# Row sums and outputs tested on the chip, with a general softmax path behind a branch at the end

## The chip, the core and the metric

The kernel runs on one core of a Trainium2 chip. The core has five engines that run side by side, each through its own instructions in order, and wait for each other by semaphores: TensorE (PE; its weight loads are listed as PEld), VectorE (DVE), ScalarE (ACT), GpSimd (POOL) and SyncE (SP, which only issues transfers and waits). The metric is the device time of one execution in microseconds; the numbers given are medians of several runs. One further execution is recorded by the hardware profiler; its span runs from the first to the last instruction of the program.

## The reference

Attention with keys that are also the values, pooled 4x4 from an image and projected, followed by a gated feed-forward block on every token.

```
q  [4, 12288, 128], kv [4, 384, 32, 128], w_sr [128, 128]
w_gate, w_val [128, 1536], w_out [1536, 128]

kv_pool = kv.reshape(B, H//4, 4, W//4, 4, C).mean(axis=(2, 4))
k = v = kv_pool.reshape(B, -1, C) @ w_sr              # 768 keys per image
s = (q @ k.T) / sqrt(C)
s = s - s.max(-1, keepdims=True)
a = exp(s);  a /= a.sum(-1, keepdims=True) + 1e-9
x = a @ v
out = (maximum(x @ w_gate, 0) * (x @ w_val)) @ w_out   # float32, [49152, 128]
```

## The kernel before

**Mathematics.** The kernel takes no maximum off the scores: it computes exp of the scaled scores in fp16 as it finds them, leaves the rows unnormalised through the values and both projections, and multiplies the output by the square of the inverse row sum, since gate and value each carry one factor of it. That is right as long as the scores are moderate.

**Tiles.** A tile is 512 tokens; there are NT = 96, in groups of GRP = 4, 24 tiles to each of the four images. A step k of the main loop (lines 811 to 865) works on four tiles at once in a software pipeline: scores and exp of tile k, values of tile k-2 (`kV`), the projections `v`, `y`, `g`, `h` of tile k-3 (`kF`), and the output projection of tile k-4 (`kO`). The order inside a step is written out by hand in the word lists STEADY, DRAIN and LAST (lines 100 to 111); nothing reorders it, because the schedule is manual (line 628). DRAIN serves the steps from k = 96 on, LAST the final one, k = 98. An `OPENING` list of words handles the first tiles while the first image's keys are still being built; its four lead tiles have transposed scores and get their row sums by a matmul with ones (`lead_sums`, `lead_inverse`, lines 467 to 498).

**Who does what.** For one tile, PE runs 8 score matmuls into the two-bank PSUM tile `wide` (line 397), 6 value matmuls (line 439), 12 value and 12 gate projections (lines 504, 515) and 12 output projections (line 545). ACT takes exp of a block of 128 tokens by 768 keys and has the row sum accumulated beside it into `a_sums` (line 402), and copies the value projections to fp16 (line 141 for `keep_value`). DVE does gate times value in one instruction (`gated`, line 523), the copy of the values (line 447), the reciprocal of a pair of tiles' row sums (`invert`, line 414) and a 32x32 block transpose of the output (line 553). POOL squares the inverse sums (416), spreads them over the partitions in 16 small copies a pair (423), multiplies the transposed output by them (line 558 in `out_turn`), pools the next images' keys (lines 256 to 264), and issues the loads of q and half of the output stores.

**The end.** Tiles 93 to 95 do not go through the transpose: their output projection runs token by token into PSUM (line 529), and `out_scale` multiplies there, on DVE for tile 93 and on ACT for tile 94; `out_store` stores. Tile 95 goes through `out_last`: three PSUM parts, the first two scaled by DVE (line 587), the last by ACT (line 585), each stored at once, the last from ACT's own queue. Then the program closes: SP waits for the stores, all engines meet, and the semaphores are cleared (instructions listed under line 894).

**Buffers.** `o_t` has two buffers, `o_sb` three, `wide` one. PSUM's other six banks are handed out by `bank` in the order in which they come free.

Of the kernel before, what the change touches and what calls it, by code (L numbers as in the profile page):

```python
# [9 lines left out]
FP32 = mybir.dt.float32  # L10
FP16 = mybir.dt.float16
AF = mybir.ActivationFunctionType
ALU = mybir.AluOpType
# [3 lines left out]
def kernel(  # L17
# [23 lines left out]
    nc = tc.nc  # L41

    B, N, C = q.shape
    _, H, W, _ = kv.shape
    r = 4
    J = (H // r) * (W // r)
    NJC = J // 128
    HC = H // NJC
    D_FF = moe_w_gate.shape[1]
    NFB = D_FF // 128  # L50
    T = 512
    NS = T // 128
    NST = N // T
    NT = B * NST
# [3 lines left out]
    X_SCALE = 512.0  # L58
    LEAD = GRP
    AT_BUFS = 4  # L60
    qk_scale = 1.0 / math.sqrt(C)

    assert C == 128 and N % T == 0 and J == 128 * NJC and D_FF == 128 * NFB
    assert NFB == 2 * NJC and NST % GRP == 0 and W // r == 8 and HC == 64
# [50 lines left out]
    const = ctx.enter_context(tc.tile_pool(name="const", bufs=1))  # L115
    work = ctx.enter_context(tc.tile_pool(name="work", bufs=2))
# [152 lines left out]
    sums, pixels = {}, {}  # L269
# [117 lines left out]
    def score_block(k, s):  # L387
        b = k // NST
        if s == 0:
            a16s[k] = work.tile([128, NS, J], FP16, tag="a16", bufs=4, name="a16")  # L390
            aTs[k] = work.tile([128, NJC, T], FP16, tag="aT", bufs=AT_BUFS, name="aT")
            if k % 2 == 0:
                a_sums[k // 2] = work.tile([128, 2, NS], FP32, tag="a_sums", bufs=2, name="a_sums")
        s_ps = s_banks[s] = wides[0].tile([128, 1024], FP32, tag="wide", name="wide_ps")
        qT = qTs[k // GRP][:, k % GRP * NS + s, :]
        for j0, j1 in ((0, 4), (4, NJC)):
            nc.tensor.matmul(  # L397
                s_ps[:, j0 * 128 : j1 * 128], qT, kv16[:, b, j0:j1, 0:C], start=True, stop=True
            )
# [87 lines left out]

    def lead_inverse():
        inverse = const.tile([128, NS * 4], FP32)
        nc.vector.reciprocal(inverse, x_banks.pop("turned")[:, :, 0])  # L490
        nc.vector.tensor_tensor(lead_square, inverse, inverse, op=ALU.mult)

    def lead_scales():
# [55 lines left out]
    def out_turn(k):  # L549


        o_t = work.tile([128, T], FP32, tag="o_t", bufs=2)
        nc.vector.transpose(o_t, freed(o_banks.pop(k)))  # L553
        o_sb = work.tile([128, 4, NS, 32], FP32, tag="o_sb", bufs=3)
        o_by = o_t.rearrange("t (s j c) -> t s j c", s=NS, j=4)
        to = o_sb.rearrange("t j s c -> t s j c")
        scale = scale_of(k).rearrange("t (s j o) -> t s j o", s=NS, o=1)
        nc.gpsimd.tensor_tensor(to, o_by, scale.to_broadcast([128, NS, 4, 32]), op=ALU.mult)  # L558
        del hTs[k]
        g = k // GRP  # L560
        rows = out[g * GRP * T : (g + 1) * GRP * T, :]
        moves = []
        for b in range(4):
            o_b = o_sb[32 * b : 32 * (b + 1)]
            if g == 0:
                to = rows.rearrange(
                    "(e j t i s) (b c) -> e b i j t s c", e=2, j=4, t=32, s=NS, c=32
                )
                moves += [(to[k // 2, b, k % 2, j], o_b[:, j]) for j in range(4)]
            elif g == NG - 1:  # L570
                to = rows.rearrange("(j t i s) (b c) -> b i j t s c", j=4, t=32, s=NS, c=32)
                moves += [(to[b, k % GRP, j], o_b[:, j]) for j in range(4)]
            else:
                to = rows.rearrange("(i t r) (b c) -> b i t r c", t=32, r=16, c=32)
                moves.append((to[b, k % GRP], o_b.rearrange("t j s c -> t (j s) c")))
        return moves
# [15 lines left out]
    def out_store(k, own, queue=nc.sync):  # L592
        queue.dma_start(
            out[k // GRP * GRP * T : (k // GRP + 1) * GRP * T, :].rearrange(
                "(p i s) c -> i p s c", p=128, i=GRP
            )[k % GRP][:, own], o_sbs[k][:, own],
        )
        if own.stop == NS:
            for tiles in (hTs, o_banks, o_sbs):
                del tiles[k]  # L600

    def out_last(k):
        parts = [bank([128, 2, 128]), bank([128, 1, 128]), bank([128, 1, 128])]
        owns = [slice(0, 2), slice(2, 3), slice(3, 4)]
        o_banks[k] = None

        def add(s, fb0, fb1):
            n = max(s - 1, 0)
            for fb in range(fb0, fb1):
                out_add(k, fb, s, parts[n][:, s - owns[n].start], fb == 0 and s != 1)  # L610

        def keep(n, engine, queue=nc.sync):
            out_scale(k, engine, owns[n], parts[n])
            out_store(k, owns[n], queue)

        held = NFB - 2
        add(0, 0, held)
        add(1, 0, held)
        add(2, 0, held)
        add(0, held, NFB)  # L620
        add(1, held, NFB)
        keep(0, nc.vector)
        add(2, held, NFB)
        keep(1, nc.vector)
        add(3, 0, NFB)
        keep(2, nc.scalar, nc.scalar)

    ctx.enter_context(tc.manual_schedule())

# [2 lines left out]
    make_identity(nc, ident)  # L632
    ident16 = const.tile([128, 128], FP16)
    nc.gpsimd.tensor_copy(ident16, ident)
    ones = const.tile([128, 32], FP16)
    nc.gpsimd.memset(ones, 1.0)
    lead_scale = const.tile([128, LEAD, NS * 4], FP32)
    nc.gpsimd.memset(kv16[:, :, :, 2 * C : 2 * C + 16], 1.0 / X_SCALE)

    w_sr_f32 = const.tile([128, C], FP32)  # L640
# [150 lines left out]
    def image_step(b, at, step):  # L791
        for pair in range(NJC // 2):
# [7 lines left out]
            elif since in (9, 11) and step == 1:  # L800
                turn_values_dma(b, 2 * pair + since // 11)

    for word in OPENING:
        word, _, number = word.partition("@")
        if number:
            asked.append(int(number))
        open_step(word)
        assert not asked
    usable[0] = 6
    last = NT + LAG - 1  # L810
    for k in range(LEAD + 2, last + 1):
        g, ph = divmod(k, GRP)
        if ph % 2:
            q_turn_two(g + 1, ph - 1)
        if ph:
            q_load(g + 2, [[0], [2], [3]][ph - 1])
        b = k // NST + 1
        at = k % NST - 4
        kO, kF, kV = k - LAG - 1, k - LAG, k - 2
        words = STEADY if k < NT else DRAIN if k < last else LAST  # L820
        for word in words:
            head, n = word.rstrip("0123456789"), int(word.lstrip("abcdefghijklmnopqrstuvwxyzADPT") or 0)
            if head == "o":
                out_proj(kO, n)
                if ph == 1 and n == NFB // 2:
                    q_load(g + 2, [1])
                for queue in (nc.gpsimd, nc.sync):
                    if out_moves and n >= 2:
                        queue.dma_start(*out_moves.pop())  # L829
                if spread:  # L830
                    spread_scales(*spread.pop(0))
                if b < B:
                    image_step(b, at, n)
            elif head == "oT":
                if kO < NT - 3:
                    out_moves.extend(out_turn(kO))
                elif k < last:
                    out_scale(kO, nc.vector, slice(0, NS))
                    out_store(kO, slice(0, NS))
            elif head in ("v", "y", "g", "h"):  # L840
                if kF < NT:
                    {"v": value_proj, "y": keep_value, "g": gate_proj, "h": gated}[head](kF, n)
            elif head in ("s", "e"):
                if k < NT:
                    {"s": score_block, "e": exp_block}[head](k, n)
                    if head == "e" and n % 2:
                        a_turn(k, n - 1, n + 1)
            elif head == "r":
                if LEAD < k <= NT and k % 2 == 0:
                    invert(k - 2)  # L850
                    spread += [(k - 2, j) for j in range(4)]
            elif head in ("tb", "P", "pk"):
                pair, since = divmod(at - 6 if head == "tb" else at - 8, 4)
                if b < B and 0 <= pair < NJC // 2 and since == 0:
                    if head == "tb":
                        moves.extend(turn_blocks(b, pair))
                    elif head == "P":
                        project(b, pair)
                    else:
                        keep_projected(b, pair)  # L860
            elif LEAD <= kV < NT:
                if head == "x":
                    values(kV, n)
                else:
                    keep_values(kV)
    out_scale(last - LAG - 1, nc.scalar, slice(0, NS))
    out_store(last - LAG - 1, slice(0, NS))
    out_last(last - LAG)


# [28 lines left out]
```

## Time and profile before

| | us |
|---|---|
| runs, median (lowest to highest of 3) | 1025.01 (1024.85 to 1026.36) |
| the profiled execution, its run | 1024.9 |
| its span | 1023.1 |
| PE busy | 1016.1 (99%) |
| ACT busy | 919.4 (90%) |
| DVE busy | 867.1 (85%) |
| POOL busy | 522.9 (51%) |
| PEld busy | 486.0 (48%) |

The granted TensorE clock was 1.0 throughout. How to read it: an engine's busy time counts its computing instructions, not its sequencer's waits and branches (POOL's issues of transfers are listed among its busy time here, as lines 162 and 829). Groups of instructions are named by their source line, with the tile that they write and those that they read and the shape as partitions x elements. The chain of waits is followed back from the last instruction to whatever released each one; its shares say which engine set the time. Most groups are the same in every tile: a tile's cast on ACT takes 596 ns on average, one gate-times-value on DVE 680 ns, an exp block 821 ns and its accumulator read 206 ns, the output scaling on POOL 1047 ns.

### The profile page before, as it was taken

How to read it: one execution, taken by the hardware profiler on the slowest of the kernel's cores; microseconds unless marked ns; L12 is line 12 of the kernel's file. 1: busy time of each engine (PE TensorE's matmuls, PEld its weight loads, DVE VectorE, ACT ScalarE, POOL GpSimd, SP SyncE). 2: the span in 40 equal slices, each digit the busy share in tenths (PEclk: the TensorE clock that was granted, in tenths of full speed). 3: DMA queues.
4: the chain of work that ended last, by engine and by line, in shares of the span. 5: the costliest groups of instructions: out<-in, count | busy, mean ns of one | idle time of the engine just before them, and what ended most of it. 6: DMA issues, size and time to landing. Idle time of an engine off the chain costs nothing.

```text
span 1023.1 us, 17486 instructions
## 1 busy us (share of the span) xinstructions
PE 1016.1 (99%) x5028; PEld 486.0 (48%) x5028; DVE 867.1 (85%) x1446; ACT 919.4 (90%) x1925; POOL 522.9 (51%) x1311
## 2 busy tenths in 40 slices
PE   8999999999999999999999999999999999999998
PEld 4444444444444444444444444444444444444445
DVE  4988888888888888888888888888888888888888
ACT  5999999999999999999999999999999999999986
POOL 3487857344347576544434856754434533443342
PEclk9999999999999999999999999999999999999999
DMA  9999998777898999788779899977686877767541
GB/s 320 172 170 183 187 202 145 141 124 127 138 199 159 182 189 174 130 123 145 122 135 200 167 173 199 159 131 133 127 131 114 149 120 129 124 121 123 102 87 44
DMA packets 475743, 153.48 MB, mean 150 GB/s; under 512 B 451584, under 2 KB 465920, under 8 KB 475648
## 3 DMA queue, kind: packets, MB, share of 16 engines
q1 hardware_dynamic: 453184, 126.08, 65.2%
q0 software_dynamic: 22032, 25.19, 16.4%
q10 hardware_dynamic: 432, 1.11, 0.3%
q8 instruction: 39, 0.64, 0.3%
q14 instruction: 56, 0.46, 0.2%
HBM read 53.94 MB, written 26.35 MB: 78 GB/s over the span
## 4 chain that ended last, share of the span: by engine, by line
PE 98%; DMA 1%; ACT 0%; DVE 0%; issue 0%; SPq 0%; DVEq 0%
PE bank_ps L504 24%; PE bank_ps L515 24%; PE bank_ps L545 24%; PE wide_ps L397 12%; PE bank_ps L439 12%; DMA kv_in<-in_kv_dram 1%; PE bank_ps L529 1%; PE bank_ps L456 0%; PE bank_ps L378 0%; PE wide_ps L336 0%; PE bank_ps L300 0%; PE bank_ps L314 0%; ACT aT L381 0%; PE bank_ps L474 0%; PE bank_ps L209 0%
## 5 line engine op out<-in xcount | busy, mean ns | idle before, releaser
L523 DVE SCALAR_TENSOR_TENSOR hT<-bank_ps,val 128x512 f16<-128x512 f32 x1152 | 728.2, 680 | 104.5 <-PE bank_ps L515 83.5
L141 ACT CAST val<-bank_ps 128x512 f16<-128x512 f32 x1149 | 629.1, 596 | 44.3 <-PE bank_ps L504 23.9
L504 PE MATMUL bank_ps<-xT,wv 128*128 128x512 f16 x1152 | 420.6, 379 | 0.0
L515 PE MATMUL bank_ps<-xT,wg 128*128 128x512 f16 x1152 | 376.3, 379 | 0.1
L545 PE MATMUL bank_ps<-hT,wo 128*128 128x512 f16 x1116 | 348.5, 379 | 0.0
L402 ACT ACTIVATE a<-wide_ps 128x768 f16<-128x768 f32 x368 | 302.0, 821 | 43.4 <-PE wide_ps L397 43.4
L397 PE MATMUL wide_ps<-kv,qT 128*128 128x512 f16 x736 | 179.7, 326 | 0.0
L439 PE MATMUL bank_ps<-aT,kv 128*128 128x512 f16 x552 | 178.9, 379 | 0.0
L558 POOL TENSOR_TENSOR o_sb<-o_t,scale 128x512 f32<-128x512 f32 x89 | 93.2, 1047 | 159.4 <-issue 142.0
L545 PEld LDWEIGHTS <-wo 128*128 128x128 f16 x1116 | 109.2, 98 | 131.9 <-issue 0.8
L515 PEld LDWEIGHTS <-wg 128*128 128x128 f16 x1152 | 112.7, 98 | 122.8 <-issue 0.8
L504 PEld LDWEIGHTS <-wv 128*128 128x128 f16 x1152 | 112.6, 98 | 105.5 <-issue 0.8
L423 POOL COPY scale<-square 32x8 f32<-32x8 f32 x736 | 141.2, 192 | 28.6
L416 POOL TENSOR_TENSOR square<-inverse 128x8 f32<-128x8 f32 x46 | 9.3, 202 | 248.0 <-DVE inverse L414 241.2
L829 POOL DMA_DIRECT2D out_dram<-o_sb x208 | 130.3, 632 | 9.9 <-POOL o_sb L558 7.4
L397 PEld LDWEIGHTS <-qT 128*128 128x128 f16 x736 | 72.0, 98 | 86.9 <-issue 0.2
L447 DVE CAST xT<-bank_ps 128x512 f16<-128x512 f32 x92 | 63.6, 692 | 32.0 <-PE bank_ps L439 32.0
L439 PEld LDWEIGHTS <-kv 128*128 128x128 f16 x552 | 54.0, 98 | 65.2
L402 ACT ACTIVATION_READ_ACCUMULATOR a<-wide_ps 128x1 f32 x368 | 76.0, 206 | 0.0
L553 DVE STREAM_TRANSPOSE o_t<-bank_ps 128x512 f32<-128x512 f32 x93 | 65.5, 704 | 0.0
L162 POOL DMA_DIRECT2D q<-in_q_dram x84 | 48.7, 581 | 0.3 <-issue 0.3
L256 POOL TENSOR_TENSOR s<-kv_in 128x512 f32<-128x512 f32 x36 | 45.1, 1283 | 0.7
(79 smaller groups left out, 204.9 us busy)
## 6 DMA issues: line engine op xcount, KB each, us to landing
kv_in<-in_kv_dram SPq DMA_DIRECT2D x42, 512.0 KB, 5.2
out_dram<-o_sb SPq DMA_DIRECT2D x177, 64.0 KB, 3.5
q<-in_q_dram POOLq DMA_DIRECT2D x88, 128.0 KB, 3.5
out_dram<-o_sb POOLq DMA_DIRECT2D x176, 64.0 KB, 4.1
aT<-a SPq DMA_TRANSPOSE x184, 4.4
kv_line<-in_kv_dram SPq DMA_DIRECT2D x4, 512.0 KB, 9.8
placed<-blocks SPq DMA_DIRECT2D x9, 128.0 KB, 2.4
kvT<-placed SPq DMA_DIRECT2D x36, 32.0 KB, 2.4
```

Source lines behind the costliest of these rows:

```text
L141: nc.scalar.copy(to, what)
L397: nc.tensor.matmul(s_ps[:, j0 * 128 : j1 * 128], qT, kv16[:, b, j0:j1, 0:C], start=True, stop=True)
L402: nc.scalar.activation(a16s[k][:, s, :], s_banks.pop(s)[:, 0:J], AF.Exp, scale=qk_scale, accum_out=a_sums[k // 2][:, k % 2, s : s + 1],)
L423: nc.gpsimd.tensor_copy(to[32 * b : 32 * (b + 1), :, :, j], squares[k // 2][32 * j : 32 * (j + 1)])
L439: nc.tensor.matmul(x_banks[k], kv16[:, k // NST, jc, C : 2 * C], aT[:, jc], start=first, stop=x_left[k] == 0,)
L504: nc.tensor.matmul(proj_banks["v", k, fb], wv16[:, fb * 128 : (fb + 1) * 128], xTs[k], start=True, stop=True,)
L515: nc.tensor.matmul(proj_banks["g", k, fb], wg16[:, fb * 128 : (fb + 1) * 128], xTs[k], start=True, stop=True,)
L523: nc.vector.scalar_tensor_tensor(hTs[k][:, fb, :], freed(proj_banks.pop(("g", k, fb))), 0.0, vals.pop((k, fb)), op0=ALU.max, op1=ALU.mult,)
L545: nc.tensor.matmul(o_banks[k], wo16[:, fb, :], hTs[k][:, fb, :], start=first, stop=o_left[k] == 0)
L553: nc.vector.transpose(o_t, freed(o_banks.pop(k)))
L558: nc.gpsimd.tensor_tensor(to, o_by, scale.to_broadcast([128, NS, 4, 32]), op=ALU.mult)
L829: queue.dma_start(*out_moves.pop())
```

## The change

The kernel now keeps every row's sum and tests on the chip whether its short cut was allowed, and has a second, general path for inputs where it was not.

- All row sums go to one constant tile `row_sums` (96 tiles x 4 sums per partition) instead of rotating buffers; the lead tiles' sums are copied there by POOL.
- After each tile's output is scaled, POOL adds one column of every 32 of it to a running tile `seen`, so that an infinity or a NaN stays visible. Tiles 93 and 94 are added in `out_store`.
- At the end of the step before the last (`oT` of k = 97), ACT runs Relu twice over all row sums, once for sums above 32 x 768 and once for sums below 768 / 8, and accumulates what is out of range (`sums_checked`).
- In `out_last`, DVE turns those accumulators and `seen` into flags (`seen_checked`, behind the last DVE scaling), and then the last tile's own outputs (`last_checked`, behind the last ACT scaling and store). A matmul with ones counts the flags over the partitions, a DVE maximum writes one integer, and all engines load that integer into a register.
- A branch runs `general()` if it is above zero: four loops of 24 iterations which compute every tile again, with each row's maximum taken off and the projections in fp32, one tile after the other. The branch is told that the side where nothing is done is the one to fall through.

The diff, with the inner part of the general path cut:

```diff
@@ -59,6 +59,7 @@
     LEAD = GRP
     AT_BUFS = 4
     qk_scale = 1.0 / math.sqrt(C)
+    SUM_MOST, SUM_LEAST = 32.0 * J, J / 8.0
 
     assert C == 128 and N % T == 0 and J == 128 * NJC and D_FF == 128 * NFB
     assert NFB == 2 * NJC and NST % GRP == 0 and W // r == 8 and HC == 64
@@ -390,7 +391,7 @@
             a16s[k] = work.tile([128, NS, J], FP16, tag="a16", bufs=4, name="a16")
             aTs[k] = work.tile([128, NJC, T], FP16, tag="aT", bufs=AT_BUFS, name="aT")
             if k % 2 == 0:
-                a_sums[k // 2] = work.tile([128, 2, NS], FP32, tag="a_sums", bufs=2, name="a_sums")
+                a_sums[k // 2] = row_sums[:, k : k + 2]
         s_ps = s_banks[s] = wides[0].tile([128, 1024], FP32, tag="wide", name="wide_ps")
         qT = qTs[k // GRP][:, k % GRP * NS + s, :]
         for j0, j1 in ((0, 4), (4, NJC)):
@@ -487,7 +488,9 @@
 
     def lead_inverse():
         inverse = const.tile([128, NS * 4], FP32)
-        nc.vector.reciprocal(inverse, x_banks.pop("turned")[:, :, 0])
+        sums_in = x_banks.pop("turned")[:, :, 0]
+        nc.gpsimd.tensor_copy(row_sums[:, 0:LEAD].rearrange("t e s -> t (e s)"), sums_in)
+        nc.vector.reciprocal(inverse, sums_in)
         nc.vector.tensor_tensor(lead_square, inverse, inverse, op=ALU.mult)
 
     def lead_scales():
@@ -556,6 +559,9 @@
         to = o_sb.rearrange("t j s c -> t s j c")
         scale = scale_of(k).rearrange("t (s j o) -> t s j o", s=NS, o=1)
         nc.gpsimd.tensor_tensor(to, o_by, scale.to_broadcast([128, NS, 4, 32]), op=ALU.mult)
+        nc.gpsimd.tensor_tensor(
+            seen, seen, o_sb[:, :, :, 0].rearrange("t j s -> t (j s)"), op=ALU.add
+        )
         del hTs[k]
         g = k // GRP
         rows = out[g * GRP * T : (g + 1) * GRP * T, :]
@@ -595,6 +601,10 @@
                 "(p i s) c -> i p s c", p=128, i=GRP
             )[k % GRP][:, own], o_sbs[k][:, own],
         )
+        if own.stop == NS and k < NT - 1:
+            nc.gpsimd.tensor_tensor(
+                seen[:, 0:NS], seen[:, 0:NS], o_sbs[k][:, :, 0], op=ALU.add
+            )
         if own.stop == NS:
             for tiles in (hTs, o_banks, o_sbs):
                 del tiles[k]
@@ -622,8 +632,11 @@
         keep(0, nc.vector)
         add(2, held, NFB)
         keep(1, nc.vector)
+        seen_checked()
         add(3, 0, NFB)
+        o_sb = o_sbs[k]
         keep(2, nc.scalar, nc.scalar)
+        last_checked(o_sb)
 
     ctx.enter_context(tc.manual_schedule())
 
@@ -632,9 +645,19 @@
     make_identity(nc, ident)
     ident16 = const.tile([128, 128], FP16)
     nc.gpsimd.tensor_copy(ident16, ident)
+    out_of_range = const.tile([1, 1], mybir.dt.int32)
     ones = const.tile([128, 32], FP16)
     nc.gpsimd.memset(ones, 1.0)
     lead_scale = const.tile([128, LEAD, NS * 4], FP32)
+    row_sums = const.tile([128, NT, NS], FP32)
+    too_much = const.tile([128, 1], FP32)
+    nc.gpsimd.memset(too_much, -SUM_MOST)
+    seen = const.tile([128, NS * 4], FP32)
+    nc.gpsimd.memset(seen, 0.0)
+    bad = const.tile([128, 2], FP32)
+    bad16 = const.tile([128, 22], FP16)
+    enough = const.tile([128, 1], FP32)
+    nc.gpsimd.memset(enough, SUM_LEAST)
     nc.gpsimd.memset(kv16[:, :, :, 2 * C : 2 * C + 16], 1.0 / X_SCALE)
 
     w_sr_f32 = const.tile([128, C], FP32)
@@ -800,6 +823,116 @@
             elif since in (9, 11) and step == 1:
                 turn_values_dma(b, 2 * pair + since // 11)
 
+    def sums_checked():
+        past = work.tile([128, NT * NS], FP32, tag="kv_s3", bufs=2, name="past")
+        sums = row_sums.rearrange("t k s -> t (k s)")
+        nc.scalar.activation(
+            past, sums, AF.Relu, scale=1.0, bias=too_much, accum_out=bad[:, 0:1]
+        )
+        nc.scalar.activation(past, sums, AF.Relu, scale=-1.0, bias=enough, accum_out=bad[:, 1:2])
+
+    def seen_checked():
+        nc.vector.tensor_scalar(bad16[:, 0:2], bad, 0.0, None, op0=ALU.is_gt)
+        nc.vector.tensor_scalar(
+            bad16[:, 2:18], seen, 0.0, 0.0, op0=ALU.mult, op1=ALU.not_equal
+        )
+
+    def last_checked(o_sb):
+        nc.vector.tensor_scalar(
+            bad16[:, 18:22], o_sb[:, :, 0], 0.0, 0.0, op0=ALU.mult, op1=ALU.not_equal
+        )
+        count = wides[0].tile([128, 1024], FP32, tag="wide", name="count_ps")
+        nc.tensor.matmul(count[0:1, 0:22], ones[:, 0:1], bad16, start=True, stop=True)
+        nc.vector.tensor_reduce(
+            out_of_range, count[0:1, 0:22], axis=mybir.AxisListType.X, op=ALU.max
+        )
+
+    def general():
+        def ps(n, shape, dtype=FP32):
+            return psum.tile(shape, dtype, tag=f"bank{n}", bufs=1, name="general_ps")
+
...
+        for b in range(B):
+            with tc.For_i(0, N, T) as n0:
+                q32 = work.tile([128, NS, C], FP32, tag="o_t", bufs=2, name="general_q32")
+                nc.sync.dma_start(
+                    q32, q[b, bass.ds(n0, T), :].rearrange("(p s) c -> p s c", s=NS)
+                )
...
+                    s_ps = wides[0].tile([128, 1024], FP32, tag="wide", name="general_wide")
+                    for j0, j1 in ((0, 4), (4, NJC)):
+                        nc.tensor.matmul(
+                            s_ps[:, j0 * 128 : j1 * 128], qT[:, s, :], kv16[:, b, j0:j1, 0:C],
+                            start=True, stop=True,
+                        )
+                    nc.vector.tensor_reduce(
+                        top[:, 0, s : s + 1], s_ps[:, 0:J], axis=mybir.AxisListType.X, op=ALU.max
+                    )
+                    nc.vector.tensor_scalar(
+                        top[:, 1, s : s + 1], top[:, 0, s : s + 1], -qk_scale, None, op0=ALU.mult
+                    )
+                    nc.scalar.activation(
+                        a16[:, s, :], s_ps[:, 0:J], AF.Exp, scale=qk_scale,
+                        bias=top[:, 1, s : s + 1], accum_out=total[:, 0, s : s + 1],
+                    )
+                    nc.vector.reciprocal(total[:, 1, s : s + 1], total[:, 0, s : s + 1])
+                    nc.vector.tensor_scalar(
+                        a16[:, s, :], a16[:, s, :], total[:, 1, s : s + 1], X_SCALE,
+                        op0=ALU.mult, op1=ALU.mult,
+                    )
...
+                o_sb = work.tile([128, NS, 128], FP32, tag="o_sb", bufs=3, name="general_o")
+                nc.vector.tensor_copy(o_sb, o_ps)
+                nc.sync.dma_start(
+                    out[bass.ds(n0 + b * N, T), :].rearrange("(p s) c -> p s c", s=NS), o_sb
+                )
+
     for word in OPENING:
         word, _, number = word.partition("@")
         if number:
@@ -832,6 +965,8 @@
                 if b < B:
                     image_step(b, at, n)
             elif head == "oT":
+                if k == last - 1:
+                    sums_checked()
                 if kO < NT - 3:
                     out_moves.extend(out_turn(kO))
                 elif k < last:
@@ -866,6 +1001,12 @@
     out_scale(last - LAG - 1, nc.scalar, slice(0, NS))
     out_store(last - LAG - 1, slice(0, NS))
     out_last(last - LAG)
+    flag = nc.values_load(
+        out_of_range[0:1, 0:1],
+        skip_runtime_bounds_check_because="it is a count of partitions that is only compared with 0",
+    )
+    with tc.If(flag > 0, preferred_fallthrough_block=False):
+        general()
 
 
 # ---- launch: one core; inputs and outputs as the reference has them ----
```

More of the change, by code (lines that the diff above doesn't have):

```diff
@@ new lines, in last_checked @@
+    def last_checked(o_sb):
[10 more added lines that the diff above has]
+            return psum.tile(shape, dtype, tag=f"bank{n}", bufs=1, name="general_ps")
+        wide32 = [
+            work.tile([128, 2, NFB, 128], FP32, tag="hT", bufs=3, name="wide32") for _ in range(2)
+        ]
+        wo32, wv32, wg32, h32 = [w[:, n] for w in wide32 for n in range(2)]
+        nc.vector.tensor_copy(wo32, wo16)
+        for to, w16 in ((wv32, wv16), (wg32, wg16)):
+            nc.vector.tensor_copy(to, w16.rearrange("c (fb f) -> c fb f", f=128))
+        for b in range(B):
[4 more added lines that the diff above has]
+                )
+                q16 = work.tile([128, NS, C], FP16, tag="val", bufs=6, name="general_q16")
+                nc.vector.tensor_copy(q16, q32)
+                qT_ps = ps(0, [128, NS, 128], FP16)
+                for s in range(NS):
+                    nc.tensor.transpose(qT_ps[:, s, :], q16[:, s, :], ident16)
+                qT = work.tile([128, NS, 128], FP16, tag="val", bufs=6, name="general_qT")
+                nc.vector.tensor_copy(qT, qT_ps)
+                a16 = work.tile([128, NS, J], FP16, tag="a16", bufs=4, name="general_a16")
+                aT = work.tile([128, NJC, T], FP16, tag="aT", bufs=AT_BUFS, name="general_aT")
+                total = work.tile([128, 2, NS], FP32, tag="general_sums", bufs=2)
+                top = work.tile([128, 2, NS], FP32, tag="square", bufs=3, name="general_top")
+                for s in range(NS):
+                    s_ps = wides[0].tile([128, 1024], FP32, tag="wide", name="general_wide")
[19 more added lines that the diff above has]
+                    )
+                aT_flat = aT.rearrange("k j t -> k (j t)")
+                nc.sync.dma_start_transpose(
+                    aT_flat.rearrange("k (x p) -> k x p", p=128), a16.rearrange("p s j -> p (s j)")
+                )
+                a_by = aT_flat.rearrange("k (s j p) -> k j s p", s=NS, j=NJC)
+                x_ps = ps(1, [128, T])
+                for jc in range(NJC):
+                    nc.tensor.matmul(
+                        x_ps, kv16[:, b, jc, C : 2 * C], a_by[:, jc],
+                        start=jc == 0, stop=jc == NJC - 1,
+                    )
+                xT = work.tile([128, T], FP32, tag="o_t", bufs=2, name="general_xT")
+                nc.vector.tensor_scalar(xT, x_ps, 1.0 / X_SCALE, None, op0=ALU.mult)
+                o_ps = ps(5, [128, NS, 128])
+                for s in range(NS):
+                    for fb in range(NFB):
+                        tokens = xT[:, s * 128 : (s + 1) * 128]
+                        v_ps, g_ps = ps(2 + fb % 2, [128, 128]), ps(fb % 2 * 4, [128, 128])
+                        nc.tensor.matmul(v_ps, wv32[:, fb, :], tokens, start=True, stop=True)
+                        nc.tensor.matmul(g_ps, wg32[:, fb, :], tokens, start=True, stop=True)
+                        val = work.tile([128, 128], FP32, tag="val", bufs=6, name="general_val")
+                        nc.scalar.copy(val, v_ps)
+                        nc.vector.scalar_tensor_tensor(
+                            h32[:, fb, :], g_ps, 0.0, val, op0=ALU.max, op1=ALU.mult
+                        )
+                    for fb in range(NFB):
+                        nc.tensor.matmul(
+                            o_ps[:, s, :], h32[:, fb, :], wo32[:, fb, :],
+                            start=fb == 0 and s == 0, stop=fb == NFB - 1, skip_group_check=True,
+                        )
+                o_sb = work.tile([128, NS, 128], FP32, tag="o_sb", bufs=3, name="general_o")
+                nc.vector.tensor_copy(o_sb, o_ps)
+                nc.sync.dma_start(
+                    out[bass.ds(n0 + b * N, T), :].rearrange("(p s) c -> p s c", s=NS), o_sb
+                )
@@ L868 @@
     out_last(last - LAG)
+    flag = nc.values_load(
+        out_of_range[0:1, 0:1],
+        skip_runtime_bounds_check_because="it is a count of partitions that is only compared with 0",
+    )
+    with tc.If(flag > 0, preferred_fallthrough_block=False):
+        general()
 _INS = ['q', 'kv', 'w_sr', 'moe_w_gate', 'moe_w_val', 'moe_w_out']
```

## The prediction

> **What bounds the kernel now.** I read the page's chain of waits first, then the stretch table, then the end of the timeline, because the change adds work of three kinds: a little in every tile, a little in the drain, and a decision after the last output.
>
> ```profile
> PE 98%; DMA 1%; ACT 0%; DVE 0%; issue 0%; SPq 0%; DVEq 0%
> ```
>
> The chain of waits is TensorE almost alone. The stretch table (busy us of each engine) says how much room the others have:
>
> ```profile
> 60.00:100.00 40.00, 40.00 (x195) 18.89 (x194) 34.14 (x58) 36.59 (x78) 34.29 (x74) 1.00 0.94 175
> 900.00:980.00 80.00, 80.00 (x387) 37.72 (x386) 68.04 (x113) 73.34 (x156) 28.75 (x86) 1.00 0.63 110
> ```
>
> The columns behind the length are PE, PEld, DVE, ACT, POOL, clock, DMA share and GB/s. PE is busy for 40.00 of 40 us even where POOL is at its fullest (34.29) and for 80.00 of 80 later, at a granted clock of 1.00. Whatever does not make PE wait costs nothing here. So the end is what is left to read, in the timeline from 1006 us on (start, length, engine, line; in brackets the idle time before):
>
> ```profile
> 1007.34 1.07 ACT L141 CAST val<-bank_ps 128x512 f16<-128x512 f32 x2 [0.28 <-PE bank_ps L504]
> 1009.53 1.24 ACT L141 CAST val<-bank_ps 128x512 f16<-128x512 f32 x2 [1.12 <-PE bank_ps L504]
> 1011.10 6.48 ACT L141 CAST val<-bank_ps 128x512 f16<-128x512 f32 x10 [0.32 <-PE bank_ps L504]
> ...
> 1017.04 2.84 PE L529 MATMUL bank_ps<-wo,hT 128*128 128x128 f16 x48
> 1017.52 1.14 ACT L585 ACTIVATE o_sb<-bank_ps,square 128x128 f32<-128x128 f32 x4
> 1019.20 0.62 DVE L587 TENSOR_TENSOR o_sb<-bank_ps,square 128x256 f32<-128x256 f32 x2 [0.90 <-PE bank_ps L529]
> 1019.97 0.37 ACT L585 ACTIVATE o_sb<-bank_ps,square 128x128 f32<-128x128 f32 x1 [1.31 <-issue]
> 1020.37 0.36 ACTq L593 DMA_DIRECT2D out_dram<-o_sb  x1
> ```
>
> The last arithmetic ends at 1020.34 us, the last store is issued at 1020.37. What comes behind it is the closing of the program, and the instructions of line 894 show that:
>
> ```profile
> L894 SPq EVENT_SEMAPHORE  x11: 17/28/28, 1020.5 to 1023.0; - x11
> L894 SPq DRAIN  x3: 7/7/13, 1022.3 to 1022.6; - x3
> L894 POOLq EVENT_SEMAPHORE_RANGE_CLEAR  x1: 139/139/139, 1022.7 to 1022.7; - x1
> L894 PEldq EVENT_SEMAPHORE  x2: 51/51/51, 1022.5 to 1023.1; - x2
> ```
>
> (In each: durations in ns, then first and last start.) SP waits through a list of some ten semaphores for the stores to land, from 1020.5 to its drain at 1022.3; then all engines meet, the semaphores are cleared, they meet again, and the span closes at 1023.1. So 1.9 us of landing and 0.8 us of closing stand behind the last arithmetic. The run of this profile took 1024.9 us, 1.8 over its span; the median of the runs, 1025.01, is 0.1 above it.
>
> **The change part by part.**
>
> Kept row sums: the eight sums of a pair of tiles go to a slice of one tile instead of a rotating one. No instruction is added; the two-buffer wait goes away. 0, provided that slices are told apart (a rival below).
>
> POOL's adds: 93 of 128x16 behind the output scaling of line 558, 2 of 128x4 behind the last stores, one 128x16 copy and three small memsets at the start. The nearest row is the square of line 416 (128x8, 202 ns); bounds are a 128x1 memset (0.10 us) and the 128x128 add of line 264 (0.454 us). At 0.20 it is 96 x 0.20 = 19 us, POOL from 523 to about 542 us; 10 to 44 by the bounds. Behind each add stand that tile's stores, the scale copies and q loads of POOL's queue, each 0.2 us later. POOL has idle time in every tile (4.6 us ahead of one L558 near 987.6), and in its fullest stretch four tiles add 0.8 to 34.29 of 40 us. The cover is gone only if POOL falls behind by a tile, when the transposes of line 553 find no free o_t and PE runs out of banks. 0, also at 0.454 (36.1 of 40). The three memsets (0.1 us each) delay a kv memset that ended at 2.1 us, before anything that PE waits for; the copy in the lead overlaps DVE's reciprocal (0.245 us) beside it.
>
> ACT's two range tests of 128x384, put at the end of the step before the last, so ahead of the last tile's first cast at 1009.53. An ACTIVATE with an operand from SBUF takes 369 ns for 128 elements (line 585); exp (821 at 768) against cast (596 at 512) gives 0.88 ns an element; so 0.37 + 256 x 0.00088 = 0.59 us each, plus an accumulator read of which about 0.1 is not overlapped: 1.4 us for two. ACT is idle for 1.12 us just there, so the first cast is some 0.3 us late, ending at 1010.4; its reader on DVE (line 523) started only at 1010.53, behind DVE's scaling at 1009.93, and ACT has 0.32 us more before 1011.10. 0. If the new function needs its own table, the ACT_TABLE_LOAD of 1.28 us at the start of the trace comes on top, the cover is gone and about 1.1 us reaches DVE, which has no slack in the last tile (12 of line 523 in 7.77 us): 0 to +1.1, I take 0, since this trace has one table load for both exp and the scaled copies.
> The Trainium skill (ScalarE: Activation LUTs, "Table sets: the hidden batching unit") says that cheap functions, relu among them, are in every set; by that there is no second load, and the sum stays.
>
> DVE's two tests of the earlier results stand behind its last scaling, done at 1019.82; POOL's last add can end by 1018.66 + 0.05 + 0.2 = 1018.9, so nothing is late: two at about 0.18 us (128x16 on DVE: 176 ns) end at 1020.2, before the last operand exists. 0.
>
> The last test is on the path. From 1020.34: 0.06 for a semaphore and 0.18 for the 128x4 test (1020.58); 0.06 and 0.22 for a matmul as the last of line 529 (219 ns; 1020.86); 0.06 and 0.19 for the maximum (1021.11). Then all five engines load one number into a register. The trace has no such load; the cheapest register instruction is a MOVE of 39 ns, the dearest thing near it the last store, 1.7 us from issue to landing. A read of memory is nearer the second kind but has only four bytes: I take 0.9, so 1022.0. Branch: a wait's 17 to 51 ns as a floor, 0.1 taken, 1022.1. So far this is no later than the landing (1022.27). What now counts is what the branch adds behind itself:
> 1. SP's list of waits, ten steps with its drain, now comes behind the branch. Its steps take 0.062 us each when nothing holds them (1022.08 to 1022.27): 0.65 us.
> 2. The skipped block advances semaphores, so the skipping side must bring them to the same state: from none to some 18 at 0.06, 1.1 us, possibly a meeting and clearing of its own (0.8). I take 0.5.
> 3. Code: the general path is some hundred instructions an engine, four times unrolled. If it lies between the branch and the closing, engines jump over it and fetch. The page's queues show how code comes:
>
> ```profile
> q8 instruction: 39, 0.64, 0.3%
> q14 instruction: 56, 0.46, 0.2%
> ```
>
> That is 16 KB packets of about 1.3 us (0.3% of 16 x 1023 us, over 39) and 8 KB ones of 0.6, fetched ahead so that no wait shows. A jump would expose a packet and its way, up to the 1.7 us of the last store: 0 to 3 us. I take 1.5, nearest to a packet by itself, since both sides of the branch meet again behind the general code wherever it lies.
>
> Sum: 1022.1 + 1.5 + 0.65 + 0.5 + 0.85 of closing = 1025.6, against 1023.1: +2.5, and on the median 1027.5.
> Ends: all of it hidden, +0.1; load 1.7, fetch 3, pads 1.1, own meeting 0.8: 1021.1 + 1.7 + 0.1 + 3 + 0.65 + 1.1 + 0.8 + 0.85 = 1029.3, +6.2 (1031.2).
> The Trainium skill (Runtime: NRT & Kernel Launch, "Instruction fetch mechanics") says that fetching ahead is sequential only and that a taken branch out of the two-page window stalls on the fetch; no row here shows a branch.
> The Trainium skill (DMA: Bandwidth & Descriptors, "Latency and other measured facts") gives a register load a floor of about 0.6 us; by that the sum is 0.3 lower, 1027.2.
>
> **Rivals.**
> *Straight through.* The branch falls through and the closing lies next to it, no fetch: 1022.1 + 0.65 + 0.5 + 0.85 = 1024.1, +1.0: 1026.0, not slower by what can be told. For it: the branch is told which side to prefer, and the landing hides 1.9 us. Against: one block must still lie somewhere, and the shorter side has to come back to it. It decides as long as fetch, pads and waits behind 1022.1 stay under 2.2 us (1023.1 + 2.05 - 0.85 - 1022.1); the forecast has 2.65.
> *Slices not told apart.* If the one tile of sums is one object to the dependencies, exp of a tile waits for a reciprocal of line 414 of another pair. ACT has 0.9 us of idle time per 10.4 us tile (3.41 of 40); losing 0.5 us per pair on PE gives 46 x 0.5 = 23 us, 1048. For it: one tile of 96 columns; against: other parts of the kernel write slices of kv16 while reading others, and PE stays at 40.00 of 40.
> *The test fires.* Then the loop recomputes all 96 tiles, far over 1500 us; sums near 768 lie inside 96 and 24576. Negligible.
>
> **How the numbers follow.** Forecast (+2.1 to +6) 0.56; straight through (+0.2 to +2) 0.38; slices or a late POOL 0.03; all hidden or slightly faster 0.03. A measurement of this kernel tells 0.2%, 2.05 us, from no change, so slower is above 1027.06: 0.57, within 0.40 and faster 0.03, since nothing on the path is taken away. The range reaches from nearly hidden to the upper end: 1025.3 to 1031.2.
>
> **What would show it.** Right: PE still 40.00 of 40 in the same stretches; POOL near 542 us; one table load; last arithmetic of the output within 0.3 us of 1020.34; the DVE maximum near 1021.1; line 894's waits starting after the branch and the span near 1025.6, with a hole between flag and closing. Wrong: SP's drain still at 1022.3 to 1022.9 (straight through), ACT or DVE idle before exp or line 523 (slices), a last cast later than 1017.6 (table load), or the hole being over 3 us.

## The result: 4.7 us slower, all of it behind the last arithmetic

| | before | after |
|---|---|---|
| runs, median (lowest to highest) | 1025.09 us (1024.85 to 1026.36) | 1029.82 us (1029.73 to 1030.25) |
| span of the profiled execution | 1023.1 us | 1027.5 us |
| ratio | | 1.0043, 95% interval 1.0032 to 1.0054 |

So the kernel is slower by 0.43%, 4.7 us by the medians and 4.4 by the spans. Two lines of the stretch table of the changed kernel (length, then busy us of PE, PEld, DVE, ACT and POOL, clock, DMA share, GB/s) answer to those shown of before:

```profile
60.00:100.00 40.00, 40.00 (x195) 18.83 (x193) 34.13 (x58) 36.80 (x78) 36.11 (x80) 1.00 0.92 178
900.00:980.00 80.00, 80.00 (x388) 37.76 (x387) 68.03 (x112) 73.27 (x155) 30.35 (x93) 1.00 0.63 111
```

POOL has 1.8 us more in the fullest stretch; PE is busy for 40.00 of 40 and 80.00 of 80 us as before. The steady part pays nothing. In the timeline of the end, first ACT alone, then all engines (start, length, engine, line):

```profile
1008.58 0.63 ACT L829 ACTIVATE past<-row_sums,too_much 128x384 f32<-128x384 f32 x1
...
1009.33 0.62 ACT L832 ACTIVATE past<-row_sums,enough 128x384 f32<-128x384 f32 x1
...
1009.95 1.11 ACT L142 CAST val<-bank_ps 128x512 f16<-128x512 f32 x2
1011.38 6.48 ACT L142 CAST val<-bank_ps 128x512 f16<-128x512 f32 x10 [0.32 <-PE bank_ps L507]
```

```profile
1020.25 0.37 ACT L591 ACTIVATE o_sb<-bank_ps,square 128x128 f32<-128x128 f32 x1 [1.31 <-POOL seen L605]
...
1020.65 0.17 DVE L841 TENSOR_SCALAR bad<-o_sb 128x4 f16<-128x4 f32 x1 [0.40 <-ACT o_sb L591]
1020.88 0.17 PE L845 MATMUL count_ps<-bad,ones 128*1 128x22 f16 x1 [0.71 <-DVE bad L841]
1021.09 0.17 DVE L846 TENSOR_REDUCE out_of_range<-count_ps 1x1 int32<-1x22 f32 x1 [0.26 <-PE count_ps L845]
```

The range tests fill ACT's old gap, and the ten casts behind them take 6.48 us as before, 0.28 us later (1011.38 against 1011.10). That 0.28 is in every later line. Nearly all of it is there from the start: the first loads of the images landed later in this execution, and DVE's first instruction on them starts at 9.19 us (8.93 before). A kernel with the same opening (the first experiment) has it at 8.93 again. The integer is there at 1021.26. What follows is no engine's work, so it has to be read from the lines of the sources 1004 (register load), 1008 (branch) and 1035 (closing), with durations in ns (min/median/max), then first and last start:

```profile
L1004 SPq TENSOR_LOAD <-out_of_range x1: 486/486/486, 1021.3 to 1021.3; - x1
...
L1004 DVEq TENSOR_LOAD <-out_of_range x1: 547/547/547, 1021.3 to 1021.3; - x1
```

```profile
L1008 SPq EVENT_SEMAPHORE  x8: 17/17/17, 1022.0 to 1022.5; - x8
L1008 SPq COMPARE_BRANCH  x2: 43/50/57, 1021.8 to 1022.6; - x2
L1008 ACTq COMPARE_BRANCH  x2: 38/48/58, 1021.8 to 1022.0; - x2
...
L1008 PEldq COMPARE_BRANCH  x2: 95/2096/4097, 1021.9 to 1022.2; - x2
L1008 DVEq COMPARE_BRANCH  x2: 51/53/55, 1021.9 to 1022.1; - x2
```

```profile
L1035 SPq EVENT_SEMAPHORE  x14: 17/28/28, 1025.8 to 1027.4; - x14
...
L1035 SPq DRAIN  x3: 7/7/13, 1026.6 to 1026.9; - x3
L1035 ACTq DRAIN  x2: 8/46/84, 1025.2 to 1026.9; - x2
L1035 DVEq DRAIN  x2: 10/34/59, 1025.5 to 1026.9; - x2
L1035 PEldq DRAIN  x2: 8/8/8, 1026.4 to 1027.0; - x2
```

Every engine has two branches: one that falls through (the engine goes on with the next instruction), then one that jumps over the general path. SP advances eight semaphores between them and is through its second branch at 1022.66; its next instruction, the first wait of the closing, starts at 1025.8: a hole of 3.2 us in which it does nothing. ACT's is 3.1 us (1022.06 to 1025.16), DVE's 3.3 (1022.16 to 1025.49), and PE's is recorded as a branch of 4.1 us. SP then goes through its list of waits (0.76 us) to its first drain at 1026.59, PE arrives at 1026.43, and the closing of 0.89 us ends the span. POOL, which computes nothing in the general path, is in its closing at 1022.39 and has no hole.

While the others stand still, code arrives. These are the code packets between 1022 and 1025.5 us (count, MB, share), q8 being PE's queue and q14 that of the others; between 1015 and 1022 there is none:

```profile
q8 instruction: 1, 0.02, 3.3%
q14 instruction: 4, 0.03, 3.1%
```

So of the 4.4 us of the spans 3.2 are SP's hole and 0.3 the opening. The load, the branch and its semaphores end at 1022.66 and cost next to nothing, since SP would have waited for the landing until then anyway (its last drain ahead of the meeting was at 1022.34 before, 1022.62 with the shift of 0.28). But SP's list of waits, which ran under the landing before, now stands behind the branch, and that is most of the rest. The page counts 41 code packets on the queue of PE's code (39 before) and 64 on that of the others (56 before).

### The profile page after: what moved, and what is told of

It reads as the page before. It is cut to its first block, busy times and chain, and to the rows that moved or that the text cites. A ratio compares the mean times of both kernels' runs of the same rounds, so it can differ in the third digit from the quotient of the medians.

```text
span 1027.5 us, 17628 instructions
## 1 busy us (share of the span) xinstructions
PE 1016.7 (99%) x5029; PEld 486.5 (47%) x5029; DVE 867.4 (84%) x1450; ACT 919.6 (90%) x1929; POOL 544.8 (53%) x1410
## 4 chain that ended last, share of the span: by engine, by line
PE 98%; DMA 1%; ACT 0%; DVE 0%; issue 0%; SPq 0%; POOL 0%; DVEq 0%; POOLq 0%
PE bank_ps L507 24%; PE bank_ps L518 24%; PE bank_ps L548 23%; PE wide_ps L398 12%; PE bank_ps L440 12%; DMA kv_in<-in_kv_dram 1%; PE bank_ps L532 1%; PE bank_ps L457 0%; PE bank_ps L379 0%; PE wide_ps L337 0%; PE bank_ps L301 0%; PE bank_ps L315 0%; ACT aT L382 0%; PE bank_ps L475 0%; PE bank_ps L210 0%
```

## The experiments

Each kernel is the changed one with the edit shown; differences are of medians against the kernel before, measured beside it: 1025.34 us in the first four, 1025.11 in the next four, 1025.35 in the last. A "hole" is the time between an engine's last branch and its next instruction, or a branch of PE that is itself recorded as that long.

**Tests alone.** Load and branch are taken out.

```diff
-    flag = nc.values_load(...)
-    with tc.If(flag > 0, preferred_fallthrough_block=False):
-        general()
```

> Row sums, POOL adds, ACT and DVE tests and the count are kept; the register load, the branch and the general path are left out. Fetch theory (the jump over the general code costs 3 to 4 us, load, pads and waits the rest): the count ends near 1021.3 us, under the landing of the last store, so +0 to +0.4 us over before. Rival 'the tests cost' (POOL's adds or ACT's tests delay the stream): +1 us or more stays.

Measured: 1025.29 us, ratio 0.9995 (0.9986 to 1.0005), span 1023.1. The closing of this kernel, SP's drain:

```profile
L1029 SPq DRAIN  x3: 7/7/13, 1022.2 to 1022.5; - x3
```

SP drains at 1022.2, as before the change (1022.3): the count, done by 1020.9, lies under the landing of the last store. The kept sums, 95 adds on POOL, the range tests and the count together cost nothing that can be told. What the changed kernel loses stems from load, branch and what stands behind the branch.

**A tiny body.** The branch stays, the code that it skips goes.

```diff
     def general():
...
-        wide32 = [
...
+        nc.vector.memset(bad, 0.0)
```

> Load and branch stay as they are, but the skipped block holds one small memset in place of the general path. Fetch theory: the target lies in code that is there already, no fetch of 3 to 4 us; load 0.5, pads of SP 0.6 and its waits 0.8 stay: about 3 us under the changed kernel, +1.2 to +1.9 over before. Rival 'any branch costs' (a taken jump empties the engine whatever its distance): +4 to +5 us as with the full path.

Measured: 1026.27 us, +0.9, ratio 1.0005 (0.9996 to 1.0015), span 1024.1. Branch and closing:

```profile
L928 PEldq COMPARE_BRANCH  x2: 95/207/319, 1021.4 to 1021.6; - x2
```

```profile
L955 SPq EVENT_SEMAPHORE  x14: 17/28/28, 1021.7 to 1024.0; - x14
...
L955 POOLq DRAIN  x3: 46/103/1622, 1021.6 to 1023.8; - x3
L955 SPq DRAIN  x3: 7/7/13, 1022.4 to 1023.5; - x3
```

PE's longest branch is 0.32 us instead of 4.1, and SP goes on at 1021.7, 0.15 us behind its own. Load and two branches are there as before, so 'any branch costs' falls: it is the code that is jumped over. The result is even below the 1.2 to 1.9 that I expected. This body needs none of SP's eight semaphores, but that is not what sets the time: the closing now waits for POOL's drain, 1.62 us from 1021.6 on, which ends at 1023.27, and SP, at its second drain at 1022.5, would have been ahead of it with some 0.6 us of semaphores too.

**One image.** A quarter of the code to skip.

```diff
-        for b in range(B):
+        for b in range(1):
             with tc.For_i(0, N, T) as n0:
```

> The general path keeps the loop of one image and leaves out those of three, a quarter of the skipped code; it is not executed. Fetch theory: SP, ACT and DVE jump over some 10 to 60 instructions and find the target there, so their holes of 3.1 to 3.4 us go; PE jumps over several hundred and still fetches for about 4 us, and ends last: 0 to 0.4 us under the changed kernel, +4.2 to +4.7 over before. Theory 'SP alone sets it': 2 us or more under the changed kernel. Rival 'any branch costs': all holes stay.

Measured: 1028.68 us, +3.3, ratio 1.0031 (1.0020 to 1.0041), span 1027.2. Branch and closing:

```profile
L1008 PEldq COMPARE_BRANCH  x2: 87/2004/3922, 1022.0 to 1022.3; - x2
```

```profile
L1035 SPq EVENT_SEMAPHORE  x14: 17/28/28, 1022.8 to 1027.1; - x14
...
L1035 ACTq DRAIN  x2: 8/46/85, 1022.6 to 1026.6; - x2
L1035 DVEq DRAIN  x2: 10/24/37, 1022.8 to 1026.6; - x2
...
```

The holes of SP, ACT and DVE are gone (they reach the closing at 1022.6 to 1022.8), PE's is still 3.9 us, and so the span is only 0.3 us shorter: three engines wait for the fourth. That PE is the one left fits the length of its code: where the path is executed (the run with the lowered limit, below), one pass of the loop has some 620 instructions on PE, 126 on DVE, 111 on ACT and 37 on SP. The holes came out as the fetch theory has them, the time did not: the runs gained 1.1 us on the changed kernel, more than the span and more than the 0 to 0.4 that I expected, and where the rest comes from stays open.

**A hint for the target.** The path is put next to the branch, so that there is one jump, and all engines are told its target ahead of the last tile's output.

```diff
-    out_last(last - LAG)
+    with tc.block():
+        tc.mark_branch_hint_location("over", "LikelyTaken", engines=list(mybir.ALL_ENGINES))
+        out_last(last - LAG)
...
-    with tc.If(flag > 0, preferred_fallthrough_block=False):
+    with tc.If(flag > 0, preferred_fallthrough_block=True, label="over"):
```

> The full general path, its side put next to the branch, so that the branch itself is the taken jump, and a prefetch hint for its target on all five engines ahead of the last tile's output, in a block of its own. Fetch theory: the target is fetched while PE still multiplies; holes of 3 to 4 us shrink to under 0.5 us: +1.2 to +2.2 over before. If the hint does nothing, or its fetch is thrown out again: +4.5 to +5.2, holes as before. Rival 'any branch costs': the same +4.5 to +5.2.

Measured: 1029.81 us, +4.5, ratio 1.0040 (1.0027 to 1.0052). Branch, hints, and code packets of PE's queue between 1015 and 1022 us (count, MB, share):

```profile
L1010 SPq EVENT_SEMAPHORE  x8: 17/17/17, 1025.8 to 1026.4; - x8
...
L1010 PEldq COMPARE_BRANCH  x1: 482/482/482, 1022.1 to 1022.1; - x1
```

```profile
L1037 PEldq BRANCH_PREFETCH_HINT  x1: 45/45/45, 1016.9 to 1016.9; - x1
L1037 ACTq BRANCH_PREFETCH_HINT  x1: 50/50/50, 1018.1 to 1018.1; - x1
...
L1037 SPq BRANCH_PREFETCH_HINT  x1: 60/60/60, 1019.6 to 1019.6; - x1
```

```profile
q8 instruction: 1, 0.02, 1.2%
```

The total is that of 'the hint does nothing', but the lines tell another story: PE's branch is down to 0.48 us, and a code packet came for it before the branch, which the changed kernel does not have in that stretch. SP still goes on only at 1025.8, and no packet came for the other engines in time. The new place of the path alone does not do it: SP, ACT and DVE have it too and keep their holes. The hint helped one engine, and the end stayed with the others.

**Both together.** The short path of one image, with the hint on PE alone.

```diff
-        for b in range(B):
+        for b in range(1):
...
+        tc.mark_branch_hint_location("over", "LikelyTaken", engines=[mybir.EngineType.PE])
```

> The shortened path of one image (three images' loops are left out, and the path is not executed), the path's side next to the branch, and the prefetch hint on PE alone. In one_image only PE's hole of 3.9 us was left, and in hint_block PE's hole had gone to 0.5 us, so the two together should leave no hole: SP's list of waits ends near 1023.7 us, +1.2 to +1.8 over before, 1.8 us or so under one_image. If the hint only moves the fetch, +3 as one_image.

Measured: 1026.21 us, +1.1, ratio 1.0010 (1.0000 to 1.0019), span 1024.4. The branch:

```profile
L1010 SPq EVENT_SEMAPHORE  x3: 17/17/17, 1022.3 to 1022.4; - x3
...
L1010 PEldq COMPARE_BRANCH  x1: 482/482/482, 1021.8 to 1021.8; - x1
```

No hole over 0.6 us is left. A code packet of q8 starts at 1017.6, behind the hint at 1016.6, so this queue is PE's. The time is 2.5 us under the short path without the hint, somewhat more than the 1.8 expected. Of the two edits, one had gained 1.1 us on the changed kernel and the other nothing; together they gain 3.6.

**Hints placed earlier.** The full path, next to the branch as in the two kernels above, all five engines told four steps before the end.

```diff
+    ending = ExitStack()
     for k in range(LEAD + 2, last + 1):
+        if k == last - 4:
+            ending.enter_context(tc.block())
+            tc.mark_branch_hint_location("over", "LikelyTaken", engines=list(mybir.ALL_ENGINES))
...
-    with tc.If(flag > 0, preferred_fallthrough_block=False):
+    with tc.If(flag > 0, preferred_fallthrough_block=True, label="over"):
```

> The full path with hints on all five engines, placed four steps (some 40 us) before the end instead of ahead of the last tile's output. Theory: a hint is acted on only when its engine next crosses from one code packet to the next; SP, ACT and DVE crossed none between hint and branch in hint_block, PE crossed one. Then engines that cross now (two or three of them, at 987 to 995 us) have the target early and lose their hole; PE crosses twice and may have thrown it out again, hole back to about 4 us: +3 to +5 in all. Rival 'hints work on PE only': ACT, DVE and SP keep their holes of 3 us or more, with no code packet for them before the branch.

Measured: 1029.80 us, +4.7, ratio 1.0046 (1.0028 to 1.0064). The branch's semaphores, each engine's first instruction behind the jump:

```profile
L1013 SPq EVENT_SEMAPHORE  x8: 17/17/17, 1026.0 to 1026.5; - x8
...
L1013 ACTq EVENT_SEMAPHORE  x1: 17/17/17, 1022.5 to 1022.5; - x1
L1013 PEldq EVENT_SEMAPHORE  x1: 51/51/51, 1022.5 to 1022.5; - x1
L1013 DVEq EVENT_SEMAPHORE  x1: 21/21/21, 1022.7 to 1022.7; - x1
```

ACT and DVE are now behind the branch at 1022.5 and 1022.7 as well; so 'hints work on PE only' falls. PE kept its gain, against the expectation. SP alone still has its 3.9 us hole, and the total has not moved.

**The complete path, shorter.** One loop over the images around the loop over the tiles; the images' keys and values go through DRAM, since the loop needs them by a running index. The path stands next to the branch and PE alone is told ahead of the last tile's output, as in both together.

```diff
-        for b in range(B):
+        with tc.For_i(0, B, 1) as b:
+            kvb = work.tile([128, NJC, 2 * C], FP16, tag="kv_in", bufs=2, name="general_kv")
+            nc.sync.dma_start(kvb, kept[bass.ds(b, 1)].rearrange("o p (j c) -> p (o j) c", j=NJC))
             with tc.For_i(0, N, T) as n0:
```

> The general path complete, but as one loop over the images around the loop over the tiles (its keys and values go through DRAM and back), so that the code to be skipped is a quarter, with the hint on PE. Fetch theory: as one_image_hint, +1.2 to +2.0 over before, some 3 us under the changed kernel. Rival 'any branch costs': +4 or more.

Measured: 1029.17 us, +4.1, ratio 1.0036 (1.0019 to 1.0053): not as expected. The branch shows why:

```profile
L1021 SPq EVENT_SEMAPHORE  x8: 17/17/17, 1022.9 to 1023.5; - x8
...
L1021 ACTq EVENT_SEMAPHORE  x1: 17/17/17, 1022.9 to 1022.9; - x1
L1021 PEldq EVENT_SEMAPHORE  x1: 51/51/51, 1023.0 to 1023.0; - x1
L1021 DVEq EVENT_SEMAPHORE  x1: 21/21/21, 1026.3 to 1026.3; - x1
```

PE, ACT and SP are behind the jump by 1023, POOL too; DVE comes at 1026.3. Its code is a little longer here than with one image: the outer loop adds some eight instructions an image on DVE (the next run, where they are executed). That this took the target out of what was already there is likely, but how far that reaches was not measured. One engine is enough to give nearly everything back.

The same kernel with the limit of the sums lowered, so that the general path runs:

```diff
-    SUM_MOST, SUM_LEAST = 32.0 * J, J / 8.0
+    SUM_MOST, SUM_LEAST = 0.5 * J, J / 8.0
```

> The kernel of short with the upper limit of the row sums lowered to 0.5 x 768, so that the test fires and the general path is executed for all 96 tiles. A tile alone should take 40 to 90 us with nothing overlapped between tiles: 5 to 10 ms in all. No theory of the fetch hangs on it; it prices the branch's other side.

Measured once: 7273.63 us, so about 65 us a tile ((7273.6 - 1029.2) / 96), at a mean granted clock of 0.81.

**Short path and early hints.** As the two before together, hints on PE, ACT and DVE.

> The complete general path as one loop over the images (as in short), with the prefetch hints on PE, ACT and DVE four steps before the end (as in early_hint). In short only DVE still had a hole (3.8 us), in early_hint only SP; each is gone in the other. Theory that every engine's hole is its own fetch: no hole is left, SP's list of waits ends 1.5 to 2 us behind the branch, +1.2 to +1.8 over before, 3 us under the changed kernel. If hints and short code disturb each other (a hole moves to another engine): +4 or more, as in short.

Measured: 1026.64 us, +1.3, ratio 1.0014 (1.0005 to 1.0023), span 1024.7. Its branch and closing:

```profile
L1028 SPq EVENT_SEMAPHORE  x8: 17/17/17, 1022.2 to 1022.8; - x8
...
L1028 DVEq EVENT_SEMAPHORE  x1: 21/21/21, 1022.4 to 1022.4; - x1
```

```profile
L1055 POOLq DRAIN  x3: 50/103/1691, 1022.2 to 1024.5; - x3
L1055 SPq DRAIN  x3: 7/7/13, 1023.6 to 1024.2; - x3
```

No engine is later than 1022.4 behind the branch. The tests and the complete general path cost 1.3 us this way, 3.2 us less than in the changed kernel (1026.64 against 1029.82), and still more than the kernel before, which has neither. What is left stands in these lines: SP's eight semaphores and its waits behind the branch, and POOL's drain of 1.69 us, which ends at 1023.9, later than SP's at 1023.6.

## Why the prediction was right, and which term was too small

**The steady part costs nothing:** right. PE's stretches are the same, POOL is at 544.8 us where about 542 was forecast (an add takes 228 ns, not 200), and the kernel with the tests alone is even with the one before. So slices of the one tile of sums are told apart, and that rival falls.

**The range tests in ACT's gap:** right. They took 0.63 and 0.62 us (0.59 forecast), one table load is in the trace, and the first cast came 0.14 us late beside the shift of 0.28 (1009.95 - 1009.53 - 0.28), under the 0.3 that was hidden.

**The chain to the flag:** right, and shorter than worked out. From the last scaling's end (1020.62) to the integer (1021.26) it took 0.64 us where 0.77 was forecast, and the register load 0.49 to 0.55 us where 0.9 was taken between 0.04 and 1.7. The Trainium skill (DMA: Bandwidth & Descriptors, "Latency and other measured facts") has about 0.6 as a floor for it; the measurement is slightly under that, and decides.

**What stands behind the branch:** right in kind and too small in size. The steps on SP, forecast and measured:

| step | forecast, us | measured, us |
|---|---|---|
| branch and semaphores of the skipping side | 0.1 + 0.5 | 0.8 (1021.84 to 1022.66) |
| fetch behind the jump | 1.5 (0 to 3) | 3.2 on SP (3.1 ACT, 3.3 DVE, 4.1 PE) |
| SP's list of waits, to its first drain | 0.65 | 0.76 (twelve waits, three more than before) |
| closing, from there | 0.85 | 0.89 |

The term that failed is the fetch: I priced it by one packet and its way, with 3 us as the upper end, and it is above that end on every engine that jumped far. It makes 1.7 of the 1.9 us by which the span was missed (1025.6 forecast); 0.28 is the opening, the shorter chain and load give 0.5 back, and the longer semaphores, waits and closing take 0.4 again. The prediction itself named a hole over 3 us as a sign against it, and so it is: against the price, not the mechanism, which tiny body and one image show. That the time still lies inside the range is luck in part: the range had room for a load of 1.7 us and for a meeting of the skipping side of 0.8, and neither came.

The Trainium skill (Runtime: NRT & Kernel Launch, "Instruction fetch mechanics") says that a taken branch to code outside the fetched window has to wait for it; the trace agrees, with 3.1 to 4.1 us.

**Straight through:** it fell, and for the reason given against it. The compare does fall through, at 44 to 95 ns, but the side that it falls into has to jump over the other one.

**The test fires:** it did not; the kernel in which it does takes 7.3 ms.

## What to carry to other kernels

Here a branch that is hardly ever needed was paid for by the code that must be jumped over, on each engine separately, and the last engine set the time: look at every engine's first instruction behind the jump, since curing one hole moves nothing while another is left. Keep the skipped code short (a loop, not an unrolled list), tell the target ahead of time where it can't be short, and do both before judging either. Tests that run in gaps of idle engines and end under the landing of the last store cost nothing here.

## What the runs showed of the hardware that was not expected

A jump to code that was not there cost 3.1 to 3.9 us on SP, ACT and DVE and 3.9 to 4.1 on PE, whether PE jumped over one image's code or four. The transfer is the smaller part: in the changed kernel the packets took 0.4 to 0.5 us for the others and 1.85 for PE. The last of the others' landed at 1023.96, and ACT, DVE and SP went on at 1025.16, 1025.49 and 1025.83; what fills the time between is not in the trace.

A hint on PE brought its packet about 1.1 us later (1016.9 to 1018.0 in the trace). Hints on ACT and DVE at 1018.1 brought none before the branch, at 969.9 and 970.7 they worked, and SP's worked in neither place. The early hints brought no packet more: from 960 to 1020 us the trace has two packets of the others and three of PE, as in the changed kernel. So there the target must have come with one of these. That a hint takes effect only when the engine next fetches code would fit, but it wasn't tested by itself and stays open.

POOL's drain took 1.6 to 1.7 us behind the branch in all kernels that have one, though POOL had no work left; once the holes are gone it is what the closing waits for. Without the branch it is there too, 1.88 us long, but from 1018.7 to 1020.6, under the landing (tests alone).
